# Listing an expert's rows: the six columns of row numbers become the stationary operand, the 96 one-hot columns the moving one, and a small constant matrix turns the result

## The chip, the cores and the metric

One core of a Trainium2 chip runs the whole program. Its TensorE (PE in the profile; PEld is its loading of stationary operands), VectorE (DVE), ScalarE (ACT), GpSimd (POOL) and SyncE (SP) run their own instruction queues in order and wait for each other by semaphores. The metric is the device time of one execution in microseconds (us); three executions of the kernel before are given.

## The reference

Three stages run one after the other, all in float32:

```python
scores = scale * np.matmul(q, k.transpose(0, 1, 3, 2))     # 4 x 8 heads, 576 x 576, head dimension 64
# softmax over the 32 largest of each row, then times v; x is 2304 tokens x 512
logits = x @ w_gate                                        # 8 experts
for idx in np.argsort(-logits.flatten()):                  # a token goes to its best expert that is not full (288 each)
    ...
h = np.maximum(x[mask] @ w1[e], 0.0); out[mask] = h @ w2[e]   # per expert, 512 -> 1024 -> 512
h = x @ w_in; g = h * np.cos(h); return g @ w_out             # 512 -> 2048 -> 512
```

The change lies in the second stage: in how the kernel lists which 288 tokens went to an expert.

## The kernel before, in words

**Attention** (0 to about 505 us) handles 128 queries at a time and adds each finished pair of heads' share to the logits `k.L`.

**Search** (class `Search`, a Python generator beside the experts' work) finds expert by expert which one is full first. For each of the 8 experts it makes up to four rounds: VectorE compares all logits with 24 thresholds (L756), TensorE counts tokens by 18 small products (L784), VectorE finds the last threshold that is not too much (L788, L789), TensorE spreads that number to all partitions (L791), VectorE refines (L795).

**Place** (L835 on), one generator per expert, turns the 288 tokens of an expert into row numbers. Tokens lie as 128 partitions x 18 columns. `pos` is a token's place in the expert (0 to 287), `j` its block of 96 and `lo` its place in the block. `ob` marks the block (3 columns), and `R` (L861) is that mark times the token's number, split in a high part (number / 64) and a low part (number mod 64): 2 x 3 = 6 columns for each of the 18. `oh` (L864) is a one-hot of `lo`, built in two halves laid out as 128 partitions x 96 x 9, so that the 96 columns of one `q` lie 9 elements of bfloat16, 18 bytes, apart. Then 18 products, one for each `q`, sum into one PSUM tile (L869), and three small VectorE operations make integers of it (L872 to L874), which the gather of the expert's rows of `x` reads (`gather`, L1147, three indirect DMAs on the GpSimd queue).

**Ticks.** Instructions go out in the order in which Python writes them; nothing reorders them later. `tick()` lets each generator do one step: first what each has for TensorE (up to a `yield 1`), then what each has for the other engines. Ticks stand between the experts' products: in the first eight steps four to a step, then two. A step is 12 products of the first layer (`h`, L1170) and 12 of the second (`y`, L1185). Ahead of the first expert, `tick(1)` is called without products between until its list is there. The generator of expert r waits until r lists are done (`s.placed`), and a gather goes out at the end of the first step in which its list is done.

**Experts** (about 533 to 860 us): weights are fetched by SP, split into a high and a low float32 part by ACT (L1070) and POOL (L1073, sometimes DVE), and multiplied. DVE also narrows float64 weights there for the last stage (L1106 to L1121). **The last MLP** (to 1308 us) has products L1322 and L1370 only.

Of the kernel before, what the change touches and what calls it, by code (L numbers as in the profile page):

```python
# [21 lines left out]
EPS1 = 1.0 - 2.0 ** -24          # the float32 next below 1  # L22
BIG = 2e37
NB = 64                          # thresholds that a round of the routing's search tries
NS, NR = 24, 4                   # the same where logits are without ties, and the rounds
MAGIC = 1.5 * 2.0 ** 23
INV2PI = 1.0 / (2.0 * math.pi)
C1 = 6.28125                     # 2 pi = C1 + C2, k * C1 exact
C2 = 2.0 * math.pi - 6.28125
PASSES = ((0, 0), (0, 1), (1, 0))  # high x high, high x low, low x high  # L30

B, H, S, D = 4, 8, 576, 64
NP = B * H // 2                  # pairs of heads
# [7 lines left out]
def constants(k, tmp):  # L41
# [22 lines left out]
    k.io16 = iota("io16", [128, E], [[1, E]], 16, 0)  # L64
    k.io128 = iota("io128", [128, 128], [[1, 128]], 0, 0, BF)
    # token of (partition, column): 4 columns of a batch's first 512, then the last 64 of two batches each
# [36 lines left out]
WARM = 6, 4                       # products that keep the tensor engine's clock up: at the start, and when the scores end  # L103
LAST = 8                          # so many last tiles have their exp masked by the vector engine alone
PLACES = 3                        # places of a pair's q and k
MID = 8                           # in the first steps of the experts the search has two ticks more
CI, CR = 8, 5                     # from this step on, so many quarters of an instruction of the float64 weights a step
NY = 6                            # places of stretches of y
L2 = 3                            # steps from a second layer's h to its o


class Attention:
    """Scores of 128 queries at a time (tile): two heads of a pair by 4 tiles each, and one tile of both heads' last 64."""
# [3 lines left out]
    def __init__(s, k, sb, ps, slow=False):  # L117
# [4 lines left out]
        # their places are taken again only by weights  # L122
# [27 lines left out]
    def load(s, p):  # L150
        """k and q with the head dimension on partitions; q's pair of heads apart, zeros beside each"""
# [21 lines left out]
    def qk_mm(s, j, c):  # L173
        # even tiles have the last 64 keys last, odd ones first
        p, hs, i = s.tiles[j]
        if c == 0:
            s.SP[j] = s.ps.tile([128, 2, 512], F32, name="sp", bufs=s.nsp)
        o = 64 if j % 2 == 0 else 0
        lh = s.QT[p][hs][:, i * 128:(i + 1) * 128] if hs < 2 else s.QT[p][2]
        s.nc.tensor.matmul(s.SP[j][:, c, :288], lh, s.KT[p][:, o + c * 288:o + c * 288 + 288], start=True, stop=True)  # L180
# [34 lines left out]
    def sign_exp(s, j):  # L215
        # sign(t(1-e) - s(1-e)): -1 from t on, 1 below, never 0 (t no power of 2); the sum gives the count
# [31 lines left out]
    def probs(s, j, kind):  # L248
        """exp of the kept scores; by 'a' with a minus where not kept, which the copy after the transposition drops"""
# [89 lines left out]
    @staticmethod  # L339
    def together(*gens):  # L340
        """a step of each in turn: the words of one have time to arrive while another works"""
        gens = list(gens)
        while gens:
            gens = [g for g in gens if next(g, gens) is not gens]

    def store(s, b):
        """x of a batch to DRAM"""
# [5 lines left out]
    def logits_t(s):  # L353
        """a finished pair's part of x, transposed"""
# [14 lines left out]
    def logits_m(s):  # L369
        """and its share of the logits"""  # L370
# [18 lines left out]
    def span(s):  # L389
        """from the logits of the first three batches: a range wider by a half, of which a 24th is the search's first step;  # L390
        and what is far below it"""
# [26 lines left out]
    def warm(s, n):  # L418
        """keeps the tensor engine's clock up where it would wait for long"""
# [4 lines left out]
    def run(s):  # L424
# [9 lines left out]
        # a pair is loaded in the step after the last scores of the one whose place it takes  # L434
# [3 lines left out]
        for step in range(ng + 6):  # L438
            gA, gB, gC, gD, gE, gF, gG = [step - i for i in range(7)]
            # when the scores are through, what is left goes on without a step between  # L440
# [74 lines left out]
    def run_slow(s):  # L515
        """any scores: 32 largest by 4 rounds of 8"""
        nc, sb = s.nc, s.sb
        V, A = nc.vector, nc.scalar
        for j, (p, hs, i) in enumerate(s.tiles):
# [35 lines left out]
            # v and q, k of a pair are needed until the last tile of the pair's group is done: NV = 2  # L555


def attention_flag(k, big):
    """where a row's 32nd largest was not proven: count out of 24..31, t or T tiny, negative or a power of 2"""
# [13 lines left out]
class Routing:  # L573
    """Pairs (token, expert) in descending logit: a token gets the first expert that is not full. In a phase all open
    experts take tokens down to the threshold at which the first of them is full; 64 thresholds a round find it."""
# [4 lines left out]
    def start(s):  # L580
        k, nc, sb, ps = s.k, s.nc, s.sb, s.ps
        PEe, V, A, G = nc.tensor, nc.vector, nc.scalar, nc.gpsimd
        # these few words lie apart, where no store has to end first
# [25 lines left out]
    def counts(s, m, O, th):  # L609
        """[E, NB]: the tokens from each threshold on, by best expert"""  # L610
# [9 lines left out]
    def over(s, pc):  # L620
        """[128, NB]: how many experts would overflow if all tokens from a threshold on were taken"""
# [6 lines left out]
    def take(s, m, O, G1):  # L628
        """assigns the tokens with G1 to their best experts; closes experts that are full"""
# [19 lines left out]
    def run_slow(s):  # L649
        """any logits: a token's ties by expert, the search down to neighbouring floats, ties between tokens by place"""  # L650
# [13 lines left out]
        with tc.For_i(0, E, 1):  # L664
# [7 lines left out]
            # hi: nothing is above; lo: all that is left is at or above  # L672
# [22 lines left out]
            # from hi on all; the ties in [lo, hi) as far as there is room, by place  # L695
# [24 lines left out]
class Search:  # L720
    """The same for logits without ties, beside other work: tick() is called where the tensor engine has time for a few
    products. Thresholds lie evenly over the logits' range; NS of them, NS between two of these, and so on for NR rounds
    find the one at which the first expert is full. The experts are numbered in this order, and
    each one's tokens are known as soon as it is full."""
# [8 lines left out]
    def tick(s, n=9):  # L733
        # first what the tensor engine does for all of them
# [17 lines left out]
    def compare(s, v):  # L752
        """[v >= -t] for t from 1 to NS"""
# [5 lines left out]
    def search(s):  # L759
# [7 lines left out]
        for r in range(E):  # L767
# [8 lines left out]
            else:  # L776
# [5 lines left out]
                for z in range(NR):  # L782
# [3 lines left out]
                    # thresholds at which no expert would take too many  # L786
# [34 lines left out]
            # which one was full: 16 + its number, if it was one  # L821
# [12 lines left out]
    def place(s, r, A, new):  # L834
        """the rows of x of the tokens of the expert that is number r"""  # L835
# [14 lines left out]
        pr, pt = rb[:, 176:177], rb[:96, 180:186]  # L850
# [17 lines left out]
        for q in range(18):  # L868
            PEe.matmul(pt, oh[q // 9][:, :, q % 9], R[:, q].rearrange("p a b -> p (a b)"), start=q == 0, stop=q == 17)  # L869
        yield 1  # L870
        h = sb.tile([96, 3], F32, name="ph")
        V.tensor_copy(h, pt[:, 3:])  # L872
        V.scalar_tensor_tensor(h, pt[:, :3], 64.0, h, op0=OP.mult, op1=OP.add)
        V.tensor_scalar(k.i96[:, 3 * r:3 * r + 3], h, float(NTOK - 1), None, op0=OP.min)  # L874
        s.placed += 1
        # and these tokens' places among all
# [124 lines left out]
class FFN:  # L1001
# [139 lines left out]
    def gather(s, e):  # L1141
        """x of an expert's tokens"""
        k = s.k
# [396 lines left out]
```

## Time and profile before

| | |
|---|---|
| three runs | 1317.45, 1322.13, 1332.70 us (median 1322.13) |
| profiled execution, first to last instruction (span) | 1308.3 us |
| profiled execution's own device time | not recorded apart; the three runs lie 9.2 to 24.4 us above its span |
| TensorE busy, whole span | 1170.2 us (89%) |
| VectorE busy | 1115.0 us (85%) |
| ScalarE, GpSimd busy | 784.0 us (60%), 758.2 us (58%) |
| mean granted TensorE clock | 0.926 of full |
| the 144 products of L869 | 26.0 us of TensorE, 5.3 us idle before them |

How to read it: busy shares are means over stages with different limits. The chain that ended last gives DVE 51% and PE 40% of the span; in the experts' stage it passes from one to the other every few microseconds. The granted clock has two levels here, 1.0 (2.4 GHz) and 0.5 (1.2 GHz). A group's mean duration of a pipelined product includes its latency; what it costs in a row of equal ones is the length of the whole row divided by their count.

### The profile page before, as it was taken

To read this page: it belongs to the slowest core of one execution; us is meant where nothing else is said; L and a number is where in the kernel's file an instruction comes from. 1 tells how busy PE (TensorE), PEld (TensorE's weight loads), DVE (VectorE), ACT (ScalarE), POOL (GpSimd) and SP (SyncE) were. 2 spreads that over 40 slices of the span, in tenths; PEclk is the share of its full clock that TensorE was granted. 3 is DMA by queue.
4 is the path that set the end of the run, shared out by engine and by line. 5 is a ranking of instruction groups with operands and counts; after the bars stand their busy time and mean duration, and the time that the engine had idled before them with its cause. 6 is when DMAs were issued, how large, how long until landed. Compare 5 with 4: busy or idle time off the path is not lost.

```text
span 1308.3 us, 22623 instructions
## 1 busy us (share of the span) xinstructions
PE 1170.2 (89%) x7449; PEld 1036.4 (79%) x7449; DVE 1115.0 (85%) x4001; ACT 784.0 (60%) x1503; POOL 758.2 (58%) x655
## 2 busy tenths in 40 slices
PE   6799999999899995768878888998899999999996
PEld 3677787788777785668878888997778899999995
DVE  7999999999999995776697789979999767777774
ACT  7989888889898871323334344655565545444442
POOL 5988887889887870554545466745574434211120
PEclk9989898899898897878798888999899899999998
DMA  4201121111110001444454555642332101000000
GB/s 118 54 22 43 32 66 30 31 61 36 30 30 37 2 1 69 154 124 156 122 163 147 163 162 164 210 138 73 110 116 81 57 1 42 25 25 25 26 25 28
DMA packets 61888, 98.06 MB, mean 75 GB/s; under 512 B 30912, under 2 KB 30912, under 8 KB 61248
## 3 DMA queue, kind: packets, MB, share of 16 engines
q1 hardware_dynamic: 53648, 74.47, 18.8%
q10 hardware_dynamic: 5136, 12.60, 2.7%
q0 software_dynamic: 2976, 9.44, 2.3%
q8 instruction: 61, 1.00, 0.3%
q14 instruction: 67, 0.55, 0.1%
HBM read 78.66 MB, written 17.83 MB: 74 GB/s over the span
## 4 chain that ended last, share of the span: by engine, by line
DVE 51%; PE 40%; issue 4%; ACT 1%; POOL 1%; DMA 1%; SPq 0%; DVEq 0%; POOLq 0%; ACTq 0%
PE pa L1322 10%; PE y L1370 9%; DVE C L190 8%; PE pa L1170 5%; PE y L1185 5%; PE av L303 3%; DVE w L238 3%; DVE P L257 2%; PE sp L180 2%; DVE ct L1330 2%; PE pa L869 2%; DVE C L205 2%; DVE w L233 2%; DVE w L235 1%; DVE r L1121 1%
## 5 line engine op out<-in xcount | busy, mean ns | idle before, releaser
L1322 PE MATMUL pa<-yh,wu 128*128 128x384 f32 x1152 | 224.3, 342 | 9.5 <-POOL yh L1306 4.9
L1370 PE MATMUL y<-wu,gh 128*128 128x512 f32 x864 | 222.0, 401 | 6.6 <-POOL gh L1358 6.1
L1322 PEld LDWEIGHTS pa<-yh,wu 128*128 128x128 f32 x1152 | 207.7, 191 | 21.0 <-POOL yh L1306 6.3
L226 POOL TENSOR_TENSOR W<-sg,S 128x576 f32<-128x576 bf16 x144 | 195.8, 1367 | 47.3 <-ACT sg L220 46.6
L1073 POOL TENSOR_TENSOR wu<-raw,wu 128x1024 fp32r<-128x1024 f32 x63 | 157.2, 2508 | 108.0 <-ACT wu L1070 99.8
L1370 PEld LDWEIGHTS y<-wu,gh 128*128 128x128 f32 x864 | 164.1, 192 | 39.8 <-POOL gh L1358 8.0
L180 PE MATMUL sp<-kT,qz 128*128 128x288 f32 x512 | 174.9, 432 | 9.6 <-ACT S L184 7.2
L303 PE MATMUL av<-vm,PT 128*128 128x65 f32 (+1 forms) x1216 | 153.4, 275 | 30.1 <-DVE xb L326 29.7
L303 PEld LDWEIGHTS av<-vm,PT 128*128 128x128 f32 (+1 forms) x1216 | 141.7, 191 | 38.1 <-DVE xb L326 35.4
L190 DVE MAX8 C<-S 128x8 f32<-128x72 f32 x1152 | 162.5, 215 | 5.6 <-ACT S L184 5.4
L264 POOL TENSOR_TENSOR P<-sg,E 128x576 f32<-128x576 bf16 x102 | 135.8, 1332 | 3.6
L1170 PE MATMUL pa<-xh,wu 128*128 128x288 f32 x768 | 132.1, 326 | 6.2 <-DVE hh L1177 3.8
L1354 ACT ACTIVATE gh<-cx 128x384 fp32r<-128x384 f32 x95 | 49.9, 525 | 145.1 <-DVE cx L1352 143.8
L1170 PEld LDWEIGHTS pa<-xh,wu 128*128 128x128 f32 x768 | 118.4, 212 | 13.1 <-issue 4.7
L1185 PE MATMUL y<-hh,wu 128*128 128x288 f32 x768 | 127.5, 319 | 0.0
L184 ACT ACTIVATE S<-sp 128x576 f32<-128x576 f32 x144 | 95.1, 660 | 53.2 <-PE sp L180 53.2
L272 PEld LDWEIGHTS pt<-ident,P 128*128 128x128 f32 x576 | 82.0, 148 | 52.7 <-POOL P L264 8.3
L1185 PEld LDWEIGHTS y<-hh,wu 128*128 128x128 f32 x768 | 116.8, 208 | 2.6 <-ACT r L1129 1.8
L272 PE MATMUL pt<-ident,P 128*128 128x128 f32 x576 | 112.8, 284 | 4.4 <-POOL P L264 2.0
L220 ACT ACTIVATE sg<-S,tb 128x576 bf16<-128x576 f32 x144 | 114.5, 795 | 2.7 <-DVE tb L211 2.7
L222 ACT ACTIVATE E<-S,nmx 128x576 f32<-128x576 f32 x144 | 113.8, 791 | 0.0
L1329 DVE TENSOR_SCALAR ct<-pa 128x384 f32<-128x384 f32 x95 | 52.6, 554 | 60.0 <-PE pa L1322 59.9
(247 smaller groups left out, 2307.1 us busy)
## 6 DMA issues: line engine op xcount, KB each, us to landing
raw<-in_moe_w_dram SPq DMA_DIRECT2D x63, 512.0 KB, 3.7
kT<-in_k_dram SPq DMA_DIRECT2D x16, 288.0 KB, 3.0
qz<-in_q_dram SPq DMA_DIRECT2D x32, 128.0 KB, 3.3
vm<-in_v_dram SPq DMA_DIRECT2D x32, 128.0 KB, 2.8
x<-xb SPq DMA_DIRECT2D x4, 1024.0 KB, 4.3
r<-in_moe_w_in_dram ACTq DMA_DIRECT2D x8, 512.0 KB, 4.1
r<-in_moe_w_out_dram ACTq DMA_DIRECT2D x8, 512.0 KB, 5.3
half<-in_moe_w_in_dram SPq DMA_DIRECT2D x8, 512.0 KB, 3.8
```

The costliest lines, as they stand in the source:

```text
L180: s.nc.tensor.matmul(s.SP[j][:, c, :288], lh, s.KT[p][:, o + c * 288:o + c * 288 + 288], start=True, stop=True)
L190: s.nc.vector.max(c[:, e, :], s.SS[j][:, 72 * e:72 * e + 72])
L220: A.activation(s.SG[j], s.SS[j], AF.Sign, bias=s.TB[g][:, u:u + 1], scale=-EPS1, accum_out=s.SUM[g][:, u:u + 1])
L226: s.nc.gpsimd.tensor_tensor(s.W[j], s.SG.pop(j), s.SS[j], op=OP.mult)
L264: nc.gpsimd.tensor_tensor(P, m, s.EX[j], op=OP.mult)
L272: s.nc.tensor.transpose(s.PT[j][:, i * 128:(i + 1) * 128], s.PB[j // 2][:, o + i * 128:o + (i + 1) * 128], s.k.ident)
L303: PEe.matmul(o[lo:hi, u, :], s.PT[j][:, c * 128 + lo:c * 128 + hi], t[:, a, c, :], start=c == 0, stop=False)
L1073: low()
L1170: PEe.matmul(p, w[:, a, f * 128:(f + 1) * 128], XH[e, c][:, b, :], start=n == 0, stop=n == 11)
L1185: PEe.matmul(Y[e][m], w[:, a, o + m * 128:o + (m + 1) * 128], t[:, b, :], start=f == 0 and i == 0, stop=f == 7 and i == 2)
L1322: s.nc.tensor.matmul(p, w[:, a, f * 128:(f + 1) * 128], s.YH[q, c][:, b, :], start=n == 0, stop=n == 11)
L1370: PEe.matmul(O[q][m], g[:, a, m * 128:(m + 1) * 128], w[:, b, c:c + 512], start=first and j == 0, stop=last and j == 2)
```

## The change

Six columns of `R` are now the stationary operand and the 96 strided columns of `oh` the moving one, so the sum comes out as 6 partitions x 96 instead of 96 x 6. VectorE casts it to bfloat16 (whole numbers up to 63); in the next tick one more product with the constant `k.join` (6 x 3: 64 for the high part, 1 for the low part of the same block) turns it to 96 x 3, and one VectorE operation clips it into the list. The constant is made at the start by two `iota` on GpSimd and three operations on VectorE. Comments are removed throughout, which moves line numbers (L869 becomes L876, L1147 becomes L1156, L1073 becomes L1082, L1170 becomes L1179, L1185 becomes L1194).

```diff
+    d6 = iota("d6", [6, 3], [[1, 3]], 0, -1, pool=tmp)
+    k.join = cp.tile([6, 3], BF, name="join")
+    V.tensor_scalar(d6, d6, 0.0, 64.0, op0=OP.is_equal, op1=OP.mult)
+    d7 = iota("d7", [6, 3], [[1, 3]], 3, -1, pool=tmp)
+    V.tensor_scalar(d7, d7, 0.0, None, op0=OP.is_equal)
+    V.tensor_tensor(k.join, d6, d7, op=OP.add)
...
-        pr, pt = rb[:, 176:177], rb[:96, 180:186]
+        pr, pt, pj = rb[:, 176:177], rb[:6, 232:328], rb[:96, 180:183]
...
         for q in range(18):
-            PEe.matmul(pt, oh[q // 9][:, :, q % 9], R[:, q].rearrange("p a b -> p (a b)"), start=q == 0, stop=q == 17)
+            PEe.matmul(pt, R[:, q].rearrange("p a b -> p (a b)"), oh[q // 9][:, :, q % 9], start=q == 0, stop=q == 17)
         yield 1
-        h = sb.tile([96, 3], F32, name="ph")
-        V.tensor_copy(h, pt[:, 3:])
-        V.scalar_tensor_tensor(h, pt[:, :3], 64.0, h, op0=OP.mult, op1=OP.add)
-        V.tensor_scalar(k.i96[:, 3 * r:3 * r + 3], h, float(NTOK - 1), None, op0=OP.min)
+        h = sb.tile([6, 96], BF, name="ph")
+        V.tensor_copy(h, pt)
+        yield
+        PEe.matmul(pj, h, k.join, start=True, stop=True)
+        yield 1
+        V.tensor_scalar(k.i96[:, 3 * r:3 * r + 3], pj, float(NTOK - 1), None, op0=OP.min)
         s.placed += 1
```

TensorE's queue at the end of the third list's 18 products (`yh` is the one-hot, `pR` is R, `pa` the PSUM tile, `xh`/`wu`/`hh` the experts' operands), before:

```order
L869 LDWEIGHTS yh_8715
L869 MATMUL pa_7746<-pR,yh_8715 96x6
L1170 MATMUL pa_8844<-xh,wu_8335 128x288 x3
L1170 MATMUL pa_8844<-xh,wu_8340 128x288 x3
L1170 MATMUL pa_8844<-xh,wu_8430 128x288 x3
L1170 MATMUL pa_8844<-xh,wu_8435 128x288 x3
L1185 MATMUL y_8787<-hh,wu_8516 128x288 x3
```

and now:

```order
L876 LDWEIGHTS pR
L876 MATMUL pa_7754<-yh_8723,pR 6x96
L1179 MATMUL pa_8842<-xh,wu_8343 128x288 x3
L1179 MATMUL pa_8842<-xh,wu_8348 128x288 x3
L1179 MATMUL pa_8842<-xh,wu_8438 128x288 x3
L1179 MATMUL pa_8842<-xh,wu_8443 128x288 x3
L881 LDWEIGHTS ph
L881 MATMUL pa_7754<-join,ph 96x3
L1194 MATMUL y_8795<-hh,wu_8524 128x288 x3
```

The operands have changed sides, and the added product with `join` stands a tick later, behind 12 of the experts' products.

VectorE's queue at the same place, before:

```order
L795 TENSOR_SCALAR rv<-rv,pa_7746 128x18
L756 TENSOR_TENSOR yh_7751<-rv,steps 128x432
L872 COPY ph<-pa_7746 96x3
L873 SCALAR_TENSOR_TENSOR ph<-pa_7746,ph 96x3
L874 TENSOR_SCALAR i_65<-ph 96x3
L880 SCALAR_TENSOR_TENSOR pt<-ppos,pA 128x18
L881 TENSOR_TENSOR slot<-slot,pt 128x18
L1118 TENSOR_SCALAR rt_8694<-r_8692 128x512
L1119 SCALAR_TENSOR_TENSOR r_8691<-r_8691,rt_8694 128x512
L1177 SCALAR_TENSOR_TENSOR hh<-pa_8844,hh 128x288
```

and now:

```order
L802 TENSOR_SCALAR rv<-rv,pa_7754 128x18
L763 TENSOR_TENSOR yh_7759<-rv,steps 128x432
L879 CAST ph<-pa_7754 6x96
L1127 TENSOR_SCALAR rt_8702<-r_8700 128x512
L1128 SCALAR_TENSOR_TENSOR r_8699<-r_8699,rt_8702 128x512
L883 TENSOR_SCALAR i_65<-pa_7754 96x3
L889 SCALAR_TENSOR_TENSOR pt<-ppos,pA 128x18
L890 TENSOR_TENSOR slot<-slot,pt 128x18
L1186 SCALAR_TENSOR_TENSOR hh<-pa_8842,hh 128x288
```

One operation fewer, and the one that writes the list (L883) now stands behind the two of the float64 weights and waits for TensorE. On GpSimd, the gathers of three of the eight experts (the third, fifth and seventh) stand one weight split (L1082) later than before; the others keep their place.

## Rows read from the trace of the kernel before

**Rows 1.** The page: span, and the two fullest engines.

```profile
span 1308.3 us, 22623 instructions
PE 1170.2 (89%) x7449; PEld 1036.4 (79%) x7449; DVE 1115.0 (85%) x4001; ACT 784.0 (60%) x1503; POOL 758.2 (58%) x655
```

**Rows 2.** Busy time by stretch (PE, PEld, DVE, ACT, POOL, clock): seven lists.

```profile
556.00:793.00 237.00, 198.85 (x1504) 188.18 (x1505) 183.08 (x406) 86.44 (x155) 119.81 (x60) 0.86 0.48 148
```

**Rows 3.** Chain of waits, 556 to 793 us: shares by line.

```profile
by line: PE pa L1170 14.8%; PE y L1185 13.4%; PE pa L869 8.8%; DVE r L1121 7.2%; DVE yh L756 6.5%; DVE yh L864 3.5%; DVE rt L1118 3.5%; DVE r L1113 3.3%; DVE r L1119 2.9%; DVE hh L1177 2.7%; PE pa L784 2.5%; DVE xh L1162 2.4%; DVE rv L795 2
```

**Rows 4.** The line of the 18 products, L869, and who waited for it.

```profile
L869 PEld LDWEIGHTS <-yh x144: 245/267/268, 521.1 to 791.4; 128*96 128x96 bf16 x144
L869 PE MATMUL pa<-pR,yh x144: 205/311/336, 521.1 to 791.4; 128*96 128x6 bf16 x144
...
  DVE rv L795: 18.4, 5
```

**Rows 5.** Chain of waits (start us, us, what): two lists' blocks, 12 products at each clock.

```profile
644.19 3.17 PE pa L869 x18
687.03 3.18 PE pa L869 x18
...
772.49 3.09 PE pa L1170 x12
...
819.87 1.59 PE pa L1170 x12
```

**Rows 6.** Chain of waits, later and earlier: contiguous moving and stationary columns.

```profile
501.24 1.20 PE pt L380 x10
...
1021.90 3.84 PE y L1370 x9
...
1030.46 2.10 PE pa L1322 x12
1032.57 2.09 PE y L1370 x9
```

**Rows 7.** By stretch (columns of Rows 2): blocks, and what follows them.

```profile
562.50:566.00 3.50, 3.50 (x31) 3.20 (x31) 1.46 (x7) 0.41 (x1) 1.13 (x2) 0.50 0.40 145
599.50:602.70 3.20, 3.20 (x19) 3.20 (x20) 0.01 (x1) 0.00 (x0) 0.00 (x0) 1.00 0.57 164
603.57:607.00 3.43, 3.43 (x16) 3.43 (x16) 2.11 (x8) 2.05 (x4) 2.09 (x3) 0.50 0.19 55
...
687.00:690.20 3.20, 3.20 (x20) 3.20 (x19) 0.00 (x0) 1.31 (x2) 0.00 (x0) 0.50 0.71 229
690.20:695.70 5.50, 5.50 (x24) 5.50 (x24) 2.56 (x9) 1.36 (x2) 3.24 (x3) 0.50 0.22 60
...
791.70:794.70 3.00, 3.00 (x14) 2.99 (x14) 1.62 (x10) 0.00 (x0) 0.00 (x0) 0.50 0.03 11
```

**Rows 8.** Timeline of DVE (start, us, instruction, idle before): behind the fourth block.

```profile
647.40 0.24 DVE L795 TENSOR_SCALAR rv<-rv,pa 128x18 f32<-128x18 f32 x1 [4.13 <-PE pa L869]
...
648.21 0.15 DVE L872 COPY ph<-pa 96x3 f32<-96x3 f32 x1
648.39 0.16 DVE L873 SCALAR_TENSOR_TENSOR ph<-pa,ph 96x3 f32<-96x3 f32 x1
648.58 0.17 DVE L874 TENSOR_SCALAR i<-ph 96x3 int32<-96x3 f32 x1
```

**Rows 9.** Timeline of POOL: gather and splits; of DVE at the same time.

```profile
649.02 0.92 POOL L1147 DMA_INDIRECT row<-x,i  x1 [3.41 <-DVE pt L880]
652.40 4.74 POOL L1073 TENSOR_TENSOR wu<-raw,wu 128x1024 fp32r<-128x1024 f32 x2
654.63 2.55 DVE L795 TENSOR_SCALAR rv<-rv,pa 128x18 f32<-128x18 f32 x1 [1.19 <-PE pa L791]
```

**Rows 10.** Timeline: a DVE, PE, DVE round trip ahead of the first expert.

```profile
515.47 0.16 PE L791 MATMUL pa<-rfe,ones 24*128 24x1 bf16 x1 [0.43 <-DVE rfe L789]
```

**Rows 11.** Timeline of POOL at the program's start.

```profile
1.48 0.43 POOL L47 IOTA io<- 128x3 f32 x3
```

## Prediction

> **What bounds the kernel now.** I read the page first: TensorE and VectorE share the span [rows 1], so neither's total says what a stage is worth. Next the stage that the change touches. From the second list to the last (237 us) TensorE is busy 84% and VectorE 77% [rows 2], and the chain of waits alternates between them: the experts' two products hold 28.2% of it, the 18 products of a list 8.8%, or 20.9 us [rows 3]. So nearly all of the seven blocks (7 x 3.17 = 22.2 us) [rows 5] lies on the chain. Then the line itself: in five cases VectorE sat idle, 18.4 us in all, until a block had ended [rows 4], though what it wants (the number spread by L791) was written just before; in the block at 599.5 it did nothing [rows 7]. A microsecond off a block is thus nearly a microsecond off the stage, until VectorE's own work is next. Last the clock: it is 0.5 behind each of the seven blocks (four rows shown) [rows 7]; 12 products take 3.09 us there and 1.59 at full clock [rows 5].
>
> **What a block costs, and why.** 3.17 us / 18 = 176 ns for a pair of load and product [rows 5]; the blocks at 599.5 (clock 1.0) and 687 (clock 0.5) fill the same 3.2 us [rows 7]. So TensorE's clock does not set it, and six moving columns do not either. Loads of contiguous columns are quicker: L380, with 128 of float32 and 8 moving, takes 1.20 / 10 = 120 ns, 0.94 ns a column [rows 6], against 176 / 96 = 1.83 here. What differs is the step of 18 bytes. The change gives the same strided columns to the moving side.
>
> **The sum, part by part** (against the profiled execution, span 1308.3; the median of the runs is 13.8 us above it, and I subtract from the median).
>
> *The 18 products.* No row shows a strided moving operand, so X, the cost of a new pair, is bounded. Low end: contiguous columns stream at 2.10 us / 12 / 384 = 0.456 ns and 2.09 / 9 / 512 = 0.454 [rows 6], so X = 44 ns at full clock, and 3.84 / 9 / 512 x 96 = 80 ns at half. High end: 1.83 ns a column as in the load, X = 176. Loads of six columns hide beside either. I take 176, the row nearest to it: same tile, same step, same 96 columns, and a pace that ignored TensorE's clock looks like one set by the reading of memory. The products then save nothing.
> By the Trainium skill, "SBUF — State Buffer", section "Door 1: The DMA port swizzle", full bandwidth needs repeated hits of a 16-byte line, and each access to a new line pays; 18 bytes is always a new line, whichever operand is read. The row at 1.83 ns agrees for the load; by this rule the swap saves nothing, which speaks against the change.
>
> *The clock behind the blocks.* Seven stretches of 3.0 to 5.5 us at 0.5 follow blocks in which six columns a pair went through [rows 7]; together 7 x 3.9 (mean of the four rows) = 27 us in which TensorE is always busy. At full clock they would take 27 x 1.59 / 3.09 = 14, so up to 13 us of TensorE are there. Now 96 columns a pair go through in the same time. Ends: none of the seven keeps its clock, or all. I take half, 6.5 us, and 0.6 of it for the end: between 0.4 (the experts' products' 28.2% of the chain [rows 3], 67 us, over their share of TensorE's time, some 167 of 199 us) and 1 (the products just behind a block are on it). Gain 3.9 us.
>
> *The product with join.* Eight loads of 96 contiguous columns with a product: 120 ns each as L380 [rows 6] (ends 44 and 176), 1.0 us, nearly all on TensorE's path: +0.9. Its wait: the cast stands where the copy stood, which ended 1.0 us behind its block (647.37 to 648.36) [rows 5, 8]; TensorE reaches the new product 12 of the experts' products later, 1.59 to 3.09 us, so it finds the cast done. That cover is gone if VectorE is held there (a rival below).
>
> *VectorE.* Copy, combine and clip took 0.15 + 0.16 + 0.17 us [rows 8]; cast and clip remain. The cast moves 96 elements a partition instead of 3, so 0.15 to 0.25: 0 to 0.16 us less a list, 0.6 us in all, half on the chain: -0.3. The clip waits for TensorE in the next tick, and the gathers' list comes a tick, 1.6 to 3.1 us, later. POOL stood idle before a gather already (3.41 us at 649) [rows 9]; it will wait longer, and the weight splits behind it start later. The cover is two steps, 24 products each, between gather and transposes. Three gathers go one split, 2.4 us, later: same cover. Nothing.
>
> *The first list.* Nothing runs beside it, so its latency counts: the copy and combine (0.31) become a cast (0.2) and a round trip with TensorE, 0.16 + some 0.1 of handing over [rows 10] and the load (0.1): +0.25.
>
> *The start.* Two `iota` of 0.43 / 3 = 0.14 us on POOL [rows 11], ahead of the fills that the first scores wait for: +0.3. Three small VectorE operations lie in its idle time there.
>
> Sum: -3.9 + 0.9 - 0.3 + 0.25 + 0.3 = -2.75: **1319 us**. The order of instructions shows that the change does what it says, so that it does not is no case of its own.
>
> **The rivals.**
>
> *A. The stride costs the moving side the same factor as the load.* 1.83 / 0.94 = 1.95, on 0.455 ns: X = 85 at full clock, 160 at half. For it: a moving operand streams twice as fast as a load where contiguous, so its port may fetch faster. Against: the pace of the load was in time, not in clocks. A block saves 18 x 91 = 1.64 us, seven 11.5, of which 0.91 (the blocks' 20.9 of 22.2 us on the chain, a little less as VectorE comes next) = 10.4; the clock as above, 3.9; costs 1.15 as above. 1322 - 13 = 1309.
>
> *B. The stride is free for the moving side.* X = 44, or 80 at half clock: 18 x 132 = 2.38 us a block, seven 16.6, x 0.91 = 15; the first list at half clock 18 x 96 = 1.7; the blocks being short, more of the clock stays, 5; costs 1.2. 1322 - 20.5 = 1301.5. For it: 96 contiguous columns do stream so [rows 6]. Against: the stride is what made the load slow.
> The Trainium skill, "TensorE: Matmul & The Clock Gate", section "Back-to-back issue gap", has a product's spacing as its columns at the array's clock plus 2.5 ns, with no word on strides: an estimate of 42.5 ns, this case. Rows 6 agree for contiguous columns to 6 to 9%; none is strided.
>
> *C. The new wait holds TensorE (slower).* VectorE's small operations are at times stretched while POOL splits weights: L795 took 2.55 us at 654.6 instead of 0.24, beside the splits at 652.4 [rows 8, 9]. If that hits the cast, it ends 1.0 + 2.3 = 3.3 us behind its block, TensorE stands at the product with join at 1.59, and waits 1.7 us; the experts' products are queued behind it, and VectorE's hidden layers (L1177) wait for those. Seven lists: 12 us; and each such wait may drop the clock, another 0.6 x 1.5 x 7 = 6. 1322 + 18 + 1 = 1341, or some 1330 if half the lists are hit. It decides where a split runs when the block ends. Against: at the blocks of 599.5 and 687 POOL did nothing [rows 7], since its queue waits at the gather for this very list; a gather that now stands one split later loses that shelter in three lists.
>
> **How the numbers follow.** Forecast 0.46, A 0.29, B 0.15, C 0.10. The likeliest gives 1319, with 1313 (all seven stretches keep their clock) to 1326 (none does, and the list's delay costs 2 to 3 us) as its own range. For 8 in 10 the range must take in A and most of B and the first half of C: 1300 to 1330. About 1% (13 us) is what a measurement of this kernel tells from no change. Faster by more: B nearly whole and half of A, 0.29. Slower by more: the full C, 0.04. Within: 0.67.
>
> **What would show it.** Length of 18 products over 18: near 170 to 176 ns says forecast, 80 to 95 A, 40 to 50 B; one number decides. The clock behind the blocks: 1.0 in three or four of seven stretches by the forecast. The idle time of TensorE before the product with join: near nothing; over 1 us in several lists is C. VectorE's wait at L795 behind a block (18.4 us in five) stays by the forecast, halves by A. What would make me wrong: X below 100, or a stage whose VectorE work takes over as soon as a block shrinks, so that even A or B moves the end by only a few microseconds.

## The result, and the profile after

| | before | after |
|---|---|---|
| median of 20 runs each, taken in turn | 1321.99 us (1306.90 to 1332.70) | 1328.95 us (1322.24 to 1336.89) |
| ratio, 95% interval | | 1.0067 [1.0040, 1.0094] |
| span of the profiled execution, mean clock | 1308.3 us, 0.926 | 1331.9 us, 0.915 |
| experts' stage: first product `h` to last `y` | 336.0 us | 347.3 us |

The change made the kernel 7 to 9 us slower: the medians lie 7 us apart, and the ratio, which compares undisturbed runs alone, gives 9. I had forecast 1319, 3 us faster; 1328.95 lies near the upper end of my range, on the other side of no change, and within 1% of it.

The two spans differ by 24 us and cannot be set against each other: attention, which the change does not touch, ended at 506.2 us in the profile of before, and between 510.7 and 523.9 in the profiles of the other kernels, which all share its code. So I compare the experts' stage, which begins with its own first product. Its row before, in the columns of [rows 2]:

```profile
533.47:869.47 336.00, 293.18 (x2242) 279.47 (x2241) 267.00 (x535) 139.82 (x248) 182.47 (x88) 0.89 0.50 156
```

The page of the kernel after (the lines of [rows 1]), and its experts' stage with the stretches behind the seven blocks (the columns of [rows 2, 7]):

```profile
span 1331.9 us, 22635 instructions
PE 1188.1 (89%) x7457; PEld 1036.8 (78%) x7457; DVE 1123.7 (84%) x3996; ACT 783.9 (59%) x1503; POOL 757.3 (57%) x657
```

```profile
546.59:893.87 347.28, 300.22 (x2248) 273.92 (x2247) 269.40 (x527) 138.82 (x245) 181.62 (x88) 0.88 0.49 152
...
576.10:579.50 3.40, 3.40 (x14) 2.88 (x13) 1.43 (x6) 0.62 (x1) 0.73 (x1) 0.50 0.41 146
617.00:620.40 3.40, 3.40 (x24) 2.98 (x23) 2.73 (x9) 1.26 (x2) 0.61 (x1) 1.00 0.58 154
663.90:667.30 3.40, 3.40 (x24) 2.96 (x23) 2.12 (x8) 0.00 (x0) 0.67 (x1) 1.00 0.34 134
709.10:712.50 3.40, 3.40 (x24) 2.93 (x22) 2.60 (x8) 1.20 (x2) 1.46 (x2) 1.00 0.73 242
753.90:757.30 3.40, 3.40 (x18) 2.79 (x16) 1.68 (x7) 1.74 (x5) 0.00 (x0) 0.68 0.03 12
796.80:800.20 3.40, 3.40 (x16) 3.03 (x15) 1.18 (x5) 0.20 (x1) 0.00 (x0) 0.60 0.35 134
816.40:819.80 3.40, 3.40 (x16) 3.17 (x15) 1.30 (x3) 1.36 (x2) 0.95 (x1) 0.52 0.62 190
```

The stage is 11.3 us longer. VectorE's idle time in it (stretch less busy) went from 69.0 to 77.9 us, its busy time from 267.0 to 269.4 with fewer instructions. Behind three of the seven blocks the clock stays at 1.0, where it was 0.5 behind every one [rows 7]; yet the stage's mean clock is not higher (0.88 against 0.89).

The line of the 18 products and who waited for it (as in [rows 4]):

```profile
L876 PEld LDWEIGHTS <-pR x144: 81/105/108, 532.8 to 816.2; 128*6 128x6 bf16 x144
L876 PE MATMUL pa<-yh,pR x144: 333/356/358, 533.4 to 816.3; 128*6 128x96 bf16 x144
...
  DVE rv L802: 18.3, 5
```

The same 18.3 us in five cases as before. The sixth list on TensorE's timeline (as in [rows 5]):

```profile
750.96 3.33 PE L876 MATMUL pa<-yh,pR 128*6 128x96 bf16 x18
754.22 2.54 PE L1194 MATMUL y<-hh,wu 128*128 128x288 f32 x12
756.69 0.24 PE L881 MATMUL pa<-join,ph 6*96 6x3 bf16 x1
756.85 2.61 PE L1179 MATMUL pa<-xh,wu 128*128 128x288 f32 x12
```

From one of the 18 starts to the next it is 176 ns at either clock (171 before): a block is no shorter. On VectorE's timeline, behind this block and behind the seventh (as in [rows 8]):

```profile
754.33 0.24 DVE L802 TENSOR_SCALAR rv<-rv,pa 128x18 f32<-128x18 f32 x1 [2.46 <-PE pa L876]
754.60 0.61 DVE L763 TENSOR_TENSOR yh<-rv,steps 128x432 bf16<-128x432 f32 x1
755.13 0.24 DVE L879 CAST ph<-pa 6x96 bf16<-6x96 f32 x1
755.30 0.43 DVE L1186 SCALAR_TENSOR_TENSOR hh<-pa,hh 128x288 fp32r<-128x288 f32 x1
756.96 0.16 DVE L883 TENSOR_SCALAR i<-pa 96x3 int32<-96x3 f32 x1 [1.23 <-PE pa L881]
...
761.99 4.08 DVE L802 TENSOR_SCALAR rv<-rv,pa 128x18 f32<-128x18 f32 x1 [0.88 <-PE pa L798]
...
797.50 0.40 DVE L1115 TENSOR_SCALAR rt<-r 128x512 int32<-128x512 int32 x1
800.13 0.16 DVE L883 TENSOR_SCALAR i<-pa 96x3 int32<-96x3 f32 x1 [2.22 <-PE pa L881]
800.21 0.17 DVE L889 SCALAR_TENSOR_TENSOR pt<-ppos,pA 128x18 f32<-128x18 f32 x1
```

The cast is done at 755.37, long before TensorE comes to the product with `join` at 756.69; VectorE then has one operation, reaches the clip L883 and stands: 1.23 us here, 2.22 at the next list. Who waits for the new product, and what the clip waits for, over all eight lists:

```profile
L881 PE MATMUL pa<-join,ph x8: 200/200/236, 537.1 to 820.1; 6*96 6x3 bf16 x8
...
  DVE ph L879: 1.1, 2
...
  DVE i L883: 6.6, 6
```

TensorE waited 1.1 us in all for the cast; VectorE waited 6.6 us at the clip. That wait is new. A VectorE that is late makes TensorE wait in its turn: for the search's comparison (`yh` of L756, now L763), ahead of the counting products, TensorE waited longer in the stage. Before, then after (us in all, times, longest):

```profile
PE pa L784 <- DVE yh L756: 14.6, 9, 6.5
```

```profile
PE pa L791 <- DVE yh L763: 25.7, 14, 4.7
```

GpSimd at the same place (as in [rows 9]):

```profile
757.39 1.42 POOL L1156 DMA_INDIRECT row<-x,i  x1 [6.53 <-DVE pt L889]
...
761.29 4.74 POOL L1082 TENSOR_TENSOR wu<-raw,wu 128x1024 fp32r<-128x1024 f32 x2
```

The split ends at 766.03 and VectorE's L802, 0.24 us in other places, begins beside it at 761.99 and ends at 766.07. VectorE is held by such splits in many places, before as well [rows 9]. For the comparisons I sum over VectorE's instructions in the stage what each took above the 10th percentile of its line and form in all the traces, counting excesses over 0.15 us (50 to 60 instructions, all but one or two of them beside a weight split on GpSimd): "held".

### The profile page after: what moved, and what is told of

It is laid out like the page before. It is cut to its first block, busy times and chain, and to the rows that moved or that the text cites. A ratio compares the mean times of both kernels' runs of the same rounds, so it can differ in the third digit from the quotient of the medians.

```text
span 1331.9 us, 22635 instructions
## 1 busy us (share of the span) xinstructions
PE 1188.1 (89%) x7457; PEld 1036.8 (78%) x7457; DVE 1123.7 (84%) x3996; ACT 783.9 (59%) x1503; POOL 757.3 (57%) x657
## 5 line engine op out<-in xcount | busy, mean ns | idle before, releaser
L1082 POOL TENSOR_TENSOR wu<-raw,wu 128x1024 fp32r<-128x1024 f32 x63 | 156.6, 2499 | 128.8 <-ACT wu L1079 120.3
L187 PE MATMUL sp<-kT,qz 128*128 128x288 f32 x512 | 178.5, 439 | 7.2 <-ACT S L191 5.3
L1179 PE MATMUL pa<-xh,wu 128*128 128x288 f32 x768 | 133.2, 328 | 1.7 <-DVE hh L1186 1.7
L1194 PE MATMUL y<-hh,wu 128*128 128x288 f32 x768 | 127.8, 320 | 0.0
L1179 PEld LDWEIGHTS pa<-xh,wu 128*128 128x128 f32 x768 | 119.5, 214 | 8.4 <-issue 5.5
L1194 PEld LDWEIGHTS y<-hh,wu 128*128 128x128 f32 x768 | 116.2, 208 | 7.0 <-issue 6.3
```

The costliest lines, as they stand in the source:

```text
L1082: low()
L1179: PEe.matmul(p, w[:, a, f * 128:(f + 1) * 128], XH[e, c][:, b, :], start=n == 0, stop=n == 11)
L1194: PEe.matmul(Y[e][m], w[:, a, o + m * 128:o + (m + 1) * 128], t[:, b, :], start=f == 0 and i == 0, stop=f == 7 and i == 2)
```

## The experiments

Each ratio is to the kernel before, run in turn with it on the same chip, with its 95% interval; the stage, VectorE's idle time (stage less busy), what it is held and its own work (the rest of its busy time) come from each kernel's one profile.

| kernel | ratio | stage us | idle | held | own |
|---|---|---|---|---|---|
| before | | 336.0 | 69.0 | 106.4 | 160.6 |
| after | 1.0067 [1.0040, 1.0094] | 347.3 | 77.9 | 109.8 | 159.6 |
| constants_only | 0.9991 [0.9955, 1.0026] | 337.0 | 73.4 | 103.0 | 160.6 |
| list_later | 0.9974 [0.9948, 1.0000] | 337.9 | 73.5 | 104.0 | 160.4 |
| list_two_later | 0.9993 [0.9954, 1.0031] | 337.1 | 77.1 | 99.0 | 161.0 |
| old_block_round_trip | 1.0058 [1.0031, 1.0084] | 345.6 | 79.2 | 106.0 | 160.4 |
| unread_trip | 0.9986 [0.9951, 1.0021] | 335.3 | 69.3 | 106.0 | 160.0 |
| two_round_trips | 1.0062 [1.0030, 1.0095] | 351.0 | 90.9 | 98.4 | 161.7 |
| clip_later | 0.9992 [0.9960, 1.0024] | 336.3 | 80.9 | 95.7 | 159.7 |
| done_later | 0.9977 [0.9941, 1.0012] | 336.2 | 75.4 | 100.8 | 160.0 |
| contig_old | 0.9981 [0.9956, 1.0005] | 333.6 | 50.4 | 117.3 | 165.9 |
| contig_new | 0.9985 [0.9953, 1.0016] | 335.4 | 53.2 | 117.6 | 164.6 |
| contig_new_clip_later | 0.9937 [0.9916, 0.9958] | 326.6 | 54.7 | 107.6 | 164.3 |
| pairs_old | 0.9923 [0.9884, 0.9962] | 328.1 | 51.7 | 117.1 | 159.3 |
| pairs_new | 0.9848 [0.9816, 0.9880] | 325.6 | 50.2 | 117.4 | 158.0 |
| pairs_new_clip_later | 0.9840 [0.9798, 0.9883] | 324.1 | 61.3 | 104.8 | 158.0 |
| triples_new | one run alone: 1305.93 us | 326.4 | 55.3 | 110.4 | 160.7 |

### Which part of the change costs?

**constants_only**: the kernel before with nothing but the six lines that make `k.join`.

> The kernel before with nothing of the change but the constant matrix (two iotas, three VectorE operations at the start), which nothing reads. Theory 'start' (the time is lost ahead of the first scores or in the attention, whose end came 12.3 us later in the changed kernel's trace): 1.004 to 1.008 of the kernel before. Theories 'wait', 'order' and 'block' (all in the experts' stage): 0.998 to 1.002.

Measured 0.9991 [0.9955, 1.0026]: no cost of the constants shows.

**list_later**: the kernel before, its clip one tick later, still from VectorE's own `h`.

```diff
         V.scalar_tensor_tensor(h, pt[:, :3], 64.0, h, op0=OP.mult, op1=OP.add)
+        yield
+        yield 1
         V.tensor_scalar(k.i96[:, 3 * r:3 * r + 3], h, ...)
```

> The kernel before, but each list is clipped and called done one tick later, with the old 18 products and the old three VectorE operations, and no product between: the places of the gathers, transposes and of the search's end are those of the changed kernel. Theory 'order' (these later places cost the 9 us): 1.005 to 1.009 of the kernel before. Theory 'wait' (VectorE standing at the clip for the product with join): 0.998 to 1.002, and VectorE has no idle time ahead of the clip.

Measured 0.9974. Three gathers stand one split later here, as in the change; the later list alone does not make it slower.

**old_block_round_trip**: the old 18 products, and a trip through TensorE in front of the clip.

```diff
...
         V.scalar_tensor_tensor(h, pt[:, :3], 64.0, h, op0=OP.mult, op1=OP.add)
+        yield
+        PEe.matmul(pj, k.ident[:96, :96], h, start=True, stop=True)
+        yield 1
-        V.tensor_scalar(k.i96[:, 3 * r:3 * r + 3], h, ...)
+        V.tensor_scalar(k.i96[:, 3 * r:3 * r + 3], pj, ...)
```

> The kernel before with its old 18 products (strided columns stationary), whose list is then sent through TensorE once more in the next tick (a float32 product with a 96 x 96 identity) and clipped from PSUM: the changed kernel's round trip and later list without its turned block. Theory 'wait': 1.004 to 1.009 of the kernel before, with 4 to 8 us of VectorE idle ahead of the clips, as in the changed kernel (6.6 us). Theory 'block' (the turned block itself costs, by 176 instead of 171 ns a pair and by what it does to the clock): 0.998 to 1.003.

Measured 1.0058 [1.0031, 1.0084]: as large a loss without the turned operands, and the two intervals overlap. It lies in the trip, not in the 18 products.

**unread_trip**: the same instructions in the same places, but the clip reads `h`, so nobody waits for the new product.

> old_block_round_trip, but the clip reads the combined list from SBUF as in the kernel before and nothing reads the product with the identity: TensorE does the same work at the same place (and waits for the list as there), VectorE waits for nothing. Theory 'wait': the loss of old_block_round_trip (1.0058) is gone, 0.996 to 1.002. If the product itself, or TensorE waiting for VectorE's list in front of it, is the cost: 1.004 to 1.008.

Measured 0.9986 [0.9951, 1.0021], clear of old_block_round_trip's interval. This is the cleanest pair, though the two ran on different chips, each against before. The clip's line and the stage in old_block_round_trip:

```profile
L877 DVE TENSOR_SCALAR i<-pa x8: 156/157/159, 531.4 to 811.6; 96x3 int32<-96x3 f32 x8
...
  PE pa L875: 9.4, 8
```

```profile
540.27:885.87 345.60, 300.99 (x2256) 286.82 (x2255) 266.42 (x535) 139.62 (x248) 180.34 (x88) 0.87 0.48 152
```

and the stage in unread_trip, where VectorE is never idle ahead of the clip:

```profile
543.76:879.03 335.27, 293.58 (x2256) 279.90 (x2255) 265.96 (x535) 139.64 (x248) 181.74 (x88) 0.90 0.50 156
```

VectorE does the same work (266.4 and 266.0 us busy, held 106.0 in both). With the wait it is idle 79.2 us instead of 69.3, and the stage is 10.3 us longer. The wait alone makes that; the added product on TensorE makes none of it. Half of it shows as TensorE's wait for the search's comparison, in old_block_round_trip, then in unread_trip:

```profile
PE pa L784 <- DVE yh L756: 20.9, 13, 6.4
```

```profile
PE pa L784 <- DVE yh L756: 15.8, 12, 4.8
```

**clip_later**: the change, with the clip a tick further back (for all lists but the first), so that the product has long ended.

```diff
         yield 1
+        if r:
+            yield
         V.tensor_scalar(k.i96[:, 3 * r:3 * r + 3], pj, ...)
```

> The changed kernel, but for all lists except the first the clip comes one tick after the product with join, so that VectorE finds it done. Theory 'wait': the loss is gone, 0.998 to 1.002 of the kernel before, VectorE's idle time at the clips falls from 6.6 us to under 1. Theories 'order' (lists now two ticks later) and 'block': still 1.005 to 1.010.

Measured 0.9992: the loss is gone. The idle time before the clip is not:

```profile
L885 DVE TENSOR_SCALAR i<-pa x8: 146/158/159, 533.4 to 805.2; 96x3 int32<-96x3 f32 x8
...
  PE pa L791: 10.3, 5
  PE pa L881: 0.3, 1
```

0.3 us is for the product with `join`. The 10.3 us end with the search's counting products (L791), in whose tick the clip now stands first: VectorE's next operation (L795) reads those, and in after it stood there 19.7 us in all; now it stands 14.4 there and 10.3 at the clip. So idle time over the stage is 80.9 us, more than after's 77.9; what fell is what GpSimd holds, 109.8 to 95.7, with the gathers of six lists up to two splits later than before. This edit thus moves two things at once, the clip and the gathers.

**done_later**: the change with its wait kept where it was; the mark that the list is done, and with it the gather, comes a tick later, and so do the two small operations that mark the taken tokens (L889, L890 in after), which stood right behind the clip.

```diff
         V.tensor_scalar(k.i96[:, 3 * r:3 * r + 3], pj, ...)
+        if r:
+            yield
         s.placed += 1
```

> The changed kernel with its waiting clip left in place, but each list except the first is called done a tick later, so that the gathers stand where clip_later has them. Theory 'wait' (VectorE standing at the clip): still 1.004 to 1.009 of the kernel before, 6 to 10 us idle at the clips. Theory 'gather' (clip_later won by its later gathers, which let GpSimd's weight splits go first and hold VectorE less): 0.997 to 1.002, and VectorE's operations are held by 95 to 100 us in the experts' stage as in clip_later (95.8) instead of 110.

Measured 0.9977, with the wait still there:

```profile
L883 DVE TENSOR_SCALAR i<-pa x8: 152/156/157, 532.7 to 803.6; 96x3 int32<-96x3 f32 x8
...
  PE pa L881: 8.2, 7
```

So the wait has no fixed price. Here it is paid back: held is 100.8 us against after's 109.8, idle time 75.4 against 77.9. Whether the gathers or the two operations moved from behind the clip do it, no run tells apart.

**list_two_later**: list_later with one tick more (for all lists but the first), no trip.

```diff
+        yield
+        yield 1
+        if r:
+            yield
         V.tensor_scalar(k.i96[:, 3 * r:3 * r + 3], h, ...)
```

> The kernel before with its lists clipped and done two ticks later (the first list one), no product between: only the places of clip and gathers differ from list_later. Theory 'gather': the later gathers win by themselves, 0.990 to 0.996 of the kernel before. Theory 'wait': places cost and win nothing, 0.996 to 1.001.

Measured 0.9993. Later gathers without a wait win nothing: VectorE is held 7 us less than before and idle 8 us more.

**two_round_trips**: the change with a second trip: VectorE copies `pj`, TensorE multiplies it by the identity a tick later, and the clip reads that.

```diff
...
-        V.tensor_scalar(k.i96[:, 3 * r:3 * r + 3], pj, ...)
+        V.tensor_copy(h2, pj)
+        yield
+        PEe.matmul(pk, k.ident[:96, :96], h2, start=True, stop=True)
+        yield 1
+        V.tensor_scalar(k.i96[:, 3 * r:3 * r + 3], pk, ...)
```

> The changed kernel, whose list takes a second trip through TensorE in one more tick (copied, multiplied with a 96 x 96 identity in float32, then clipped): VectorE waits twice. Theory 'wait', taken as a dose: 10 to 16 us of VectorE idle ahead of the two operations (6.6 us in the changed kernel) and 1.011 to 1.016 of the kernel before. If the first wait had only used up slack that is gone now or had moved the order once: 1.005 to 1.009, as the changed kernel.

Measured 1.0062, no more than one trip, so my price per wait was wrong. The copy's line:

```profile
L884 DVE COPY ph<-pa x8: 156/157/157, 532.9 to 817.0; 96x3 f32<-96x3 f32 x8
...
  PE pa L881: 10.7, 8
```

VectorE stood 10.7 us there and 2.1 at the clip, but the list, and so the gathers, came another tick later, and held fell to 98.4. The gathers stand behind the same splits here as in clip_later, done_later and list_two_later, which lose nothing: their places alone do not make up for a wait.

### What sets the 176 ns?

Three layouts of the one-hot, each with the new order of operands and two with the old (only the edit's line of the layout is shown). In **contig** the 96 columns of one `q` lie side by side (2 bytes apart); in **pairs** two `q` share a stretch (4 bytes apart; halves of 10 and 8 `q`); in **triples** three (6 bytes).

```diff
-        oh = [s.big(2 + h, 9 * 96, BF).rearrange("p (a b) -> p a b", b=9) for h in range(2)]
+        oh = [s.big(2 + h, 9 * 96, BF).rearrange("p (b a) -> p b a", b=9) for h in range(2)]                      # contig
+        oh = [s.big(2 + h, 192 * (5 - h), BF).rearrange("p (z a b) -> p z a b", a=96, b=2) for h in range(2)]    # pairs
+        oh = [s.big(2 + h, 9 * 96, BF).rearrange("p (z a b) -> p z a b", z=3, b=3) for h in range(2)]            # triples
...
```

**contig_old** (old operands) and **contig_new** (the change):

> The kernel before, whose one-hot is laid out 128 x 9 x 96, so that the 96 stationary columns of a product lie side by side (2 bytes apart instead of 18); VectorE then builds it with the place broadcast along the innermost axis. Theory 'step' (176 ns a pair comes from the 18 bytes between columns): a pair takes 25 to 60 ns, a list's block 0.5 to 1.1 us instead of 3.2; VectorE's one-hot takes 0.9 to 1.0 us a half instead of 0.61, 5 us more in all; 0.990 to 0.996 of the kernel before. Theory 'width' (a load of 96 bfloat16 columns is slow in itself): still 165 to 176 ns a pair, 1.002 to 1.006.

> The changed kernel with the same contiguous one-hot, now the moving operand. Theory 'step': 40 to 50 ns a pair at full clock, 80 at half; the wait at the clip stays (5 to 7 us of VectorE); 0.996 to 1.002 of the kernel before. If the moving side is slow at 96 columns for another reason than the step: 165 to 176 ns a pair and 1.008 to 1.012.

A full-clock block of contig_old, then of contig_new, by TensorE's timeline:

```profile
647.64 0.97 PE L869 MATMUL pa<-pR,yh 128*96 128x6 bf16 x18
```

```profile
654.01 0.93 PE L876 MATMUL pa<-yh,pR 128*6 128x96 bf16 x18
```

Start to start it is 45 and 42 ns at full clock, 80 at half, against 171 and 176 before: the step of 18 bytes was the cost, on either side. Yet the ratios are 0.9981 and 0.9985. VectorE now builds this one-hot in 1.05 us a half instead of 0.65 (own work 4 to 5 us more) and is held more, 117 us, though as much as in pairs below, which gain.

**contig_new_clip_later**: contig_new with clip_later's edit.

> The changed kernel with the contiguous one-hot and, but for the first list, the clip one tick after the product with join. Both costs gone: 0.990 to 0.996 of the kernel before, 6 to 9 us under contig_new by theory 'wait'. If the wait at the clip matters only beside a long block: the same as contig_new within 0.3%.

Measured 0.9937 [0.9916, 0.9958] against 0.9985 [0.9953, 1.0016], on one chip: moving the clip back pays here too.

**pairs_old** and **pairs_new**:

> The kernel before (96 columns stationary, 6 moving, no product with join) with the one-hot in pairs, 4 bytes between columns. Theory 'step' alone: a pair of load and product 45 to 80 ns, VectorE's one-hot near 0.6 us, no wait at the clip: 0.982 to 0.988 of the kernel before, as pairs_new or better. Theory 'step and clock' (96 moving columns also keep TensorE's clock up more than six do): the clock is 0.5 for 10 to 20 us longer between the first and the last list than in pairs_new (57.9 us), and 0.988 to 0.995.

> The changed kernel with the one-hot in pairs: 96 moving columns 4 bytes apart instead of 18, VectorE's operands with two neighbours innermost. Theory 'step' as a matter of lines of 16 bytes: 40 to 50 ns a pair at full clock, as if contiguous, and VectorE's one-hot near 0.6 us as before; 0.994 to 1.000 of the kernel before (the wait at the clip stays). If every step over one element is slow: 80 to 176 ns a pair, 1.003 to 1.008.

Measured 0.9923 and 0.9848, the latter the largest gain so far: 45 and 43 ns a pair of load and product, and the one-hot at 0.55 to 0.65 us a half as at first. The stage in pairs_old, then in pairs_new:

```profile
552.64:880.69 328.05, 274.85 (x2242) 260.63 (x2240) 276.38 (x534) 138.86 (x245) 181.62 (x87) 0.90 0.49 157
```

```profile
539.53:865.09 325.56, 272.95 (x2248) 256.76 (x2247) 275.38 (x527) 138.58 (x245) 181.79 (x87) 0.93 0.52 161
```

In this layout turning the operands does pay: the intervals lie apart (different chips, each against before). Why is not shown. The mean clock of 0.90 means 2 x 0.10 x 328 = 66 us at the half level, 0.93 means 46 us, and over whole runs the clock was 0.912 to 0.931 in pairs_old's nine and 0.928 to 0.937 in pairs_new's six. That is as the theory "step and clock" expected. But contig_old and contig_new differ in the same way, and neither their ratios nor their stages' clocks (0.88 and 0.89) set them apart; and list_later, no slower than before, has a stage clock of 0.87 against 0.89. The two profiled stages differ by only 2.5 us of the 9 us between the kernels' medians; pairs_old's profile is of an execution 12 us above its median, and where the rest lies, one profile of each doesn't tell. The wait at the clip is smaller than in after, 3.2 us instead of 6.6.

**pairs_new_clip_later**: both edits together, the version to beat both kernels.

> pairs_new with the clip one tick after the product with join (but for the first list): neither strided columns nor VectorE's wait. If the two costs add up: 0.979 to 0.983 of the kernel before (0.4 to 0.6% under pairs_new, as between contig_new and contig_new_clip_later). If short blocks leave VectorE time to spare: 0.984 to 0.987.

Measured 0.9840 [0.9798, 0.9883], 1302.49 us, level with pairs_new (1300.76). Either is about 1.5% faster than before and 2% faster than after. In this layout the clip's place no longer shows; in contig, whose blocks are as short, it did.

**triples_new**: the change at a step of 6 bytes.

> The changed kernel with the one-hot in threes: 96 moving columns 6 bytes apart, between the 4 of pairs_new (43 ns a pair at full clock) and the 18 of the changed kernel (176). If reading is limited to one line of 16 bytes in some 1.8 ns (176 / 96): 2.67 columns a line, 66 ns a pair at full clock. If full speed wants two columns of a line: 42 to 45 ns. If the cost grows with the step: 60 to 70 ns too, then not told apart by this run.

```profile
642.37 1.33 PE L876 MATMUL pa<-yh,pR 128*6 128x96 bf16 x18
```

66 ns start to start at full clock. Counted in the 16-byte lines that the prediction cites, 96 columns at 18 bytes touch 96 lines, 176 / 96 = 1.83 ns each; at 6 bytes they touch 36, and 36 x 1.83 = 66. At 4 bytes, 24 x 1.83 = 44: what the columns take anyway (43). One run at one more step cannot exclude another law that grows with the step; one in proportion to it would give 176 / 3 = 59.

## Why the prediction was wrong, and where it was right

**The step that failed** is the one headed VectorE: "The clip waits for TensorE in the next tick, and the gathers' list comes a tick, 1.6 to 3.1 us, later. ... Nothing." The half on the gathers held: list_later, with them in the same places, measured 0.9974. But I put the clip's own wait at nothing without a reason: I followed the gathers and the splits behind them and never asked what stands behind the clip on VectorE's own queue. There stand the mark of the taken tokens, the float64 narrowing, the hidden layers that TensorE wants next, and the search's next comparison. VectorE stood 6.6 us at the clip, and TensorE waited 25.7 us instead of 14.6 for the comparisons; in old_block_round_trip 10 us more idle time by the same means made the stage 10.3 us longer than in unread_trip. In rival C I had looked for a wait of TensorE on VectorE; the loss came from the other direction. The row that should have warned me was my own: TensorE reaches the new product 12 of the experts' products behind the block, 1.59 to 3.09 us [rows 5]. I used that time as cover for the cast; it is just as much the time VectorE may have to stand. As an estimate, seven such waits of 1.59 to 3.09 us, each less some 0.6 us of other work, would have been +7 to +17 us, and the forecast 1326 or more instead of 1319. That 1328.95 lies within my range is luck: above 1326 it was there for the first half of rival C, which did not happen, and the 2 to 3 us that it allowed for the list's delay were meant for a delay that costs nothing by itself (list_later).

**Right: X.** 176 ns, so "the products save nothing", and A (85) and B (44) fell. VectorE's wait behind the blocks stayed at 18 us as forecast. The reason was right as well: contig and pairs take the step away and the price with it. A's factor of 1.95 had compared the strided load with L380's float32 columns at 0.94 ns; contig_old's columns take at most 45 / 96 = 0.47 ns each, so the step costs the load nearly a factor of four. The Trainium skill, "SBUF — State Buffer", section "Door 1: The DMA port swizzle", has lines of 16 bytes and a penalty for each access to a new one, and the 176 ns of the change and, counted by lines, triples' 66 agree with that. It also has two hits of a line as enough for full bandwidth; triples, with 2.7 columns to a line, took 66 ns where contiguous columns took 42, and the measurement decides.

**Right in the clock, wrong in its worth.** "1.0 in three or four of seven stretches": three of seven, and three more between the levels. But the -3.9 us never reached the end. My reading, which no run tests by itself, is that TensorE runs the 12 products faster and then waits for VectorE, which sets the pace. What the runs do show is that beside the same trip the turned block is worth nothing measurable (after 1.0067, old_block_round_trip 1.0058), nor is it in clip_later (0.9992). So the factor of 0.6 that I took from shares of the chain gave the stretches a credit that did not come.

**Right: C's condition.** TensorE waited 1.1 us in all for the cast, and the cast was never stretched (0.235 to 0.247 us in the eight lists).

**Start and first list.** The first score came 0.19 us later (0.3 forecast); from the last addition to the logits to the first `h` it is 28.1 us instead of 27.3, 0.8 where I had 0.25. Both are small, and constants_only shows none of the start's at the end.

**Open.** Why later gathers pay for a wait (done_later, clip_later), though alone they win nothing (list_two_later), I can only describe. In the old layout the four kernels whose gathers stand as in clip_later are held 95.7 to 100.8 us, all others 103.0 to 109.8; but two_round_trips, one of the four, is slow all the same, with VectorE idle 90.9 us and TensorE's wait for the comparisons no longer than before (14.7 us). So the wait is shown to make the loss where nothing else moves, and what a wait costs when the gathers move with it stays open. List by list, with one profile of each kernel, I could not separate it.

## What to carry to other kernels

A round trip through another engine costs the engine that reads its result, not only those who need it: before moving a product a step back, look at what is queued behind its reader, and put the reader a step later still; here that took the loss away, though by moving the gathers as well. And ask of an operand first how many lines of memory its step touches, before turning which side it is on; here a step of 4 bytes instead of 18 brought blocks of 18 products from 3.2 us to 0.94, and only in that layout was turning the operands worth something.

## What the runs showed of the hardware that I had not expected

- A strided operand of 96 bfloat16 columns costs nearly the same as stationary (171 ns at 18 bytes) or moving (176 ns), and at either clock. About 1.83 ns for each line of 16 bytes that it touches fits 18, 6 and 4 bytes; where the columns themselves take longer (42 to 45 ns at full clock, 80 at half), the step is free.
- The layout that is best for TensorE is not best for VectorE: writing the one-hot with its value spread over the innermost 96 took 1.05 us a half, with pairs innermost 0.55 to 0.65. Pairs serve both.
- GpSimd's weight splits hold VectorE's instructions for about 100 us of a stage of 336, in 50 to 60 pieces, and between kernels with the same splits that sum moves by 22 us (95.7 to 117.6).
